# Segmented attention with memory beside a gated feed-forward: a new load order at the start, K of the first segment in two parts, recall in two halves, and a new written-out order

## Chip, core and metric

One Trainium2 chip, one core. The metric is device time of one execution in microseconds (us). Every instruction belongs to one engine: PE (TensorE; PEld is its weight load), DVE (VectorE), ACT (ScalarE), POOL (GpSimd) and SP (SyncE, which issues the transfers). Each engine runs its own queue in order.

## What is computed

The input x has 2048 rows of 512. Half A is attention with 32 heads of 16 over four segments of 512 rows, with a memory M that is carried from segment to segment; half B is a feed-forward of width 1792. A gate per row mixes the two.

```
q, k, v = x @ wq, x @ wk, x @ wv              # 32 heads of 16, 4 segments of 512
for s in range(4):
    p     = softmax(q[s] @ k[s].T * scale + causal_mask);  a_dot = p @ v[s]
    a_mem = (phi(q[s]) @ M) / (phi(q[s]) @ z + 1e-6)
    o[s]  = sigmoid(beta) * a_mem + (1 - sigmoid(beta)) * a_dot
    M, z  = M + phi(k[s]).T @ v[s],  z + phi(k[s]).sum()
a = concat(o) @ wo
b = (relu(x @ W_gate) * (x @ W_up)) @ W_down
out = sigmoid(x . gate_w) * a + (1 - sigmoid(x . gate_w)) * b
```

Inputs and outputs are bf16; phi(t) is t + 1 where t > 0 and exp(t) elsewhere.

## The kernel before, in words

**Tiling.** A unit is four pairs of heads (128 channels) of one segment: 4 units in each of the 4 segments. For each unit the kernel projects Q and K (`proj_q`, `proj_k`, transposed, 128 x 512 each, four matmuls over the four 128-row pieces of x), and for each segment four tiles of V (`proj_v`). x arrives transposed in `xT`: for segment 0 its first half of columns is turned on PE (`x0_tasks`, against an identity), its second half by a DMA transpose; later segments come by DMA transposes alone.

**Scores.** `score` (L636 and L649) runs four row tiles of PE side by side: each uses 32 rows and 128 columns of the array. A visit fills PSUM banks 0 to 3 (128 x 2048 f32), and one ACT instruction (L658) takes the exponential of all of it. The next visit writes the same banks, so it waits for that exponential. There are 72 visits: four of ordinary blocks per unit (2 matmuls in each of 4 row tiles), and one of diagonal blocks per two units (8 in each, L649). POOL masks the blocks (L687), DVE the diagonal ones (L669).

**Products and memory.** `pv` (L709) multiplies the exponentials with V in column tiles (128 rows, 32 columns of the array), `dens` (L765) and `memory` (L829) too. `recall` (L805) multiplies phi(q) with M in 16 tiles of 32 x 32, for all four units of a segment at once: 16 matmuls, each with 512 columns to stream, into four banks. `normalise` and the lines after it bring a unit's result to `oT` on DVE.

**The rest.** `ffn_tasks` makes gate and up (L478 or L482), Relu on ACT (L873) and the product on DVE (L879); `out_tile` adds `W_down` and `wo` in one bank, scales it on DVE (L905) and stores it (L910). These and the projections go through `full`: either as one matmul with 128 x 128 weights (L478), or as four with 32 columns of weights each, side by side (L482). One such quad does what one full matmul does.

**The order.** Nothing is scheduled on the chip. Every piece of work is a `Task`, in a `Plan`; the string `ORDER` gives the order in which all tasks are emitted, `UNITS` which buffer or PSUM bank each one takes. `Plan.run` walks through it. It also decides which of the two forms `full` takes: the quad form only if the last task with a mode of its own was one in column tiles.

```
            if t.eng == "PE":
                t.col = bool(t.flex) and mode == "col"
                mode = mode if t.col else t.mode
```

**The start.** `heat` (L924) keeps PE busy on constants, then the turns of x (L515), one filler matmul on zeros (L524), and Q of segment 0. The loads of SP's queue stand in this order: half of x's first rows, wq's piece 0, the DMA transpose of x's second half (L304), wq's pieces 2 and 3 (L306), wk in two halves, wv, the feed-forward weights by pieces, the rest of x. ACT's queue issues the other half of x and wq's piece 1. `LANDS` holds arrival times for the planner that made `ORDER`; the emitted kernel doesn't use them.

Of the kernel before, what the change touches and what calls it, by code (L numbers as in the profile page):

```python
# [12 lines left out]
P = 128  # L13
# [13 lines left out]
RQ = 5  # L27
RH = 14

ORDER = """  # L30
# [99 lines left out]
class Plan:  # L130

    def __init__(self):
        self.tasks, self.free = [], {}
# [9 lines left out]
    def add(self, *a, **k):  # L143
        t = Task(*a, **k)
        t.n = len(self.tasks)
        self.tasks.append(t)
        return t
# [32 lines left out]
def kernel(  # L180
# [492 lines left out]
    def attention(seg, c):  # L673
# [17 lines left out]
        if c % 2 == 0:  # L691
            diag(seg, c)
# [298 lines left out]
```

## Time and profile before

| | |
|---|---|
| time, median of 3 runs | 263.75 us (263.46 to 264.06) |
| profiled execution, span from first to last instruction | 261.6 us |
| granted TensorE clock | 0.998 |
| busy PE / DVE / ACT / POOL | 254.8 / 203.4 / 183.3 / 64.2 us |

The profiled execution has no time of its own beside its span; 2.1 us lie between the span and the median of the runs. In the views, a row of the timeline is: start, length, engine, line, operation, output from inputs, shapes, count; in brackets the idle time before and what ended it. Lengths of matmuls overlap, so the spacing of starts is what a matmul costs. About 30 of 3800 matmuls have no record, so a count can be one short.

### The profile page before, as it was taken

To read this page: it belongs to the slowest core of one execution; us is meant where nothing else is said; L and a number is where in the kernel's file an instruction comes from. 1 tells how busy PE (TensorE), PEld (TensorE's weight loads), DVE (VectorE), ACT (ScalarE), POOL (GpSimd) and SP (SyncE) were. 2 spreads that over 40 slices of the span, in tenths; PEclk is the share of its full clock that TensorE was granted. 3 is DMA by queue.
4 is the path that set the end of the run, shared out by engine and by line. 5 is a ranking of instruction groups with operands and counts; after the bars stand their busy time and mean duration, and the time that the engine had idled before them with its cause. 6 is when DMAs were issued, how large, how long until landed. Compare 5 with 4: busy or idle time off the path is not lost.

```text
span 261.6 us, 8758 instructions
## 1 busy us (share of the span) xinstructions
PE 254.8 (97%) x3769; PEld 117.2 (45%) x3798; DVE 203.4 (78%) x472; ACT 183.3 (70%) x168; POOL 64.2 (25%) x168
## 2 busy tenths in 40 slices
PE   8999999999999999999999999999999999999995
PEld 3444444454444454544444444445444344445454
DVE  2799999889896766948989868858988678788622
ACT  3199998998877788787768576878486768972000
POOL 8023462313322223322112222122122232120000
PEclk9999999999999999999999999999999999999999
DMA  7999885021311202100210500140200100230011
GB/s 193 305 289 283 214 262 109 4 43 23 84 34 43 89 25 80 36 0 3 84 21 3 95 4 26 58 142 3 80 4 23 32 5 23 98 107 3 3 43 40
DMA packets 31565, 19.71 MB, mean 75 GB/s; under 512 B 16040, under 2 KB 29992, under 8 KB 31528
## 3 DMA queue, kind: packets, MB, share of 16 engines
q1 hardware_dynamic: 31112, 18.90, 26.3%
q8 instruction: 29, 0.48, 0.8%
q10 hardware_dynamic: 416, 0.26, 0.3%
q14 instruction: 8, 0.07, 0.1%
HBM read 13.21 MB, written 2.55 MB: 60 GB/s over the span
## 4 chain that ended last, share of the span: by engine, by line
PE 90%; DVE 5%; DMA 1%; issue 1%; SPq 1%; ACT 0%; DVEq 0%; ACTq 0%
PE ps L478 54%; PE ps L482 19%; PE ps L636 8%; PE ps L709 7%; DMA wq_sb<-in_A_wq_dram 1%; PE ps L649 1%; DVE ktr L585 1%; DVE KT L588 1%; PE ps L829 1%; SPq L304 1%; DVE QT L569 0%; PE ps L765 0%; DVE T L740 0%; DVE hT L879 0%; PE ps L805 0%
## 5 line engine op out<-in xcount | busy, mean ns | idle before, releaser
L658 ACT ACTIVATE E<-ps 128x2048 bf16<-128x2048 f32 x64 | 120.1, 1877 | 32.0 <-PE ps L636 21.8
L687 POOL TENSOR_SCALAR_AFFINE_SELECT E<-E 128x256 bf16<-128x256 bf16 x128 | 55.6, 458 | 170.0 <-ACT E L658 169.9
L879 DVE TENSOR_TENSOR hT<-ps,rgr 128x512 bf16<-128x512 f32 x56 | 37.8, 684 | 13.1 <-PE ps L478 8.4
L478 PE MATMUL ps<-xT,wu_sb 128*128 128x512 bf16 x163 | 45.6, 380 | 0.7 <-issue 0.5
L873 ACT ACTIVATE rgr<-ps 128x512 bf16<-128x512 f32 x56 | 32.6, 596 | 15.3 <-PE ps L482 8.2
L478 PE MATMUL ps<-wd_sb,hT 128*128 128x512 bf16 (+1 forms) x174 | 41.7, 354 | 0.6 <-issue 0.5
L478 PE MATMUL ps<-xT,wg_sb 128*128 128x512 bf16 x149 | 40.9, 380 | 0.3
L740 DVE STREAM_TRANSPOSE T<-ps 128x512 f32<-128x512 f32 x32 | 22.2, 706 | 6.8 <-PE ps L709 6.6
L636 PE MATMUL ps<-QT,KT 32*128 32x320 bf16 (+3 forms) x512 | 25.4, 273 | 0.3
L478 PEld LDWEIGHTS <-wu_sb 128*128 128x128 bf16 x170 | 15.3, 98 | 19.4 <-issue 3.0
L478 PEld LDWEIGHTS <-hT 128*128 128x128 bf16 x178 | 15.6, 98 | 17.6 <-issue 2.1
L905 DVE TENSOR_SCALAR osr<-ps,ngcol 128x512 bf16<-128x512 f32 (+2 forms) x18 | 12.3, 691 | 13.3 <-PE ps L482 9.1
L478 PEld LDWEIGHTS <-wg_sb 128*128 128x128 bf16 x156 | 14.3, 98 | 17.8 <-issue 2.1
L709 PE MATMUL ps<-E,Vp 128*17 128x320 bf16 (+3 forms) x512 | 19.3, 273 | 0.0
L636 PEld LDWEIGHTS <-KT 32*128 32x128 bf16 x512 | 7.6, 92 | 25.7 <-issue 24.6
L658 ACT ACTIVATE Em<-ps 128x2048 bf16<-128x2048 f32 x8 | 15.0, 1874 | 5.0 <-PE ps L649 5.0
L482 PE MATMUL ps<-xT,wg_sb 128*32 128x512 bf16 x272 | 17.8, 379 | 0.0
L482 PE MATMUL ps<-wd_sb,hT 128*32 128x512 bf16 (+1 forms) x296 | 16.9, 359 | 0.0
L478 PE MATMUL ps<-wv_sb,xT 128*128 128x512 bf16 x59 | 16.7, 380 | 0.2
L478 PE MATMUL ps<-xT,wq_sb 128*128 128x512 bf16 x57 | 15.9, 382 | 0.5 <-DMA wq_sb<-in_A_wq_dram 0.4
L478 PE MATMUL ps<-xT,wk_sb 128*128 128x512 bf16 x54 | 15.3, 379 | 0.2 <-issue 0.2
L482 PE MATMUL ps<-xT,wu_sb 128*32 128x512 bf16 x216 | 15.0, 379 | 0.0
(100 smaller groups left out, 293.7 us busy)
## 6 DMA issues: line engine op xcount, KB each, us to landing
out_dram<-osr SPq DMA_DIRECT2D x15, 128.0 KB
wd_sb<-in_B_W_down_dram SPq DMA_DIRECT2D x2, 896.0 KB
xn<-in_A_x_dram SPq DMA_DIRECT2D x3, 512.0 KB
cdr<-coefs SPq DMA_DIRECT2D x6, 256.0 KB
xn<-coefs SPq DMA_DIRECT2D x6, 256.0 KB
wg_sb<-in_B_W_gate_dram SPq DMA_DIRECT2D x2, 512.0 KB
wu_sb<-in_B_W_up_dram SPq DMA_DIRECT2D x2, 512.0 KB
wg_sb<-in_B_W_gate_dram SPq DMA_DIRECT2D x2, 384.0 KB
```

The source lines that it names most:

```text
L304: nc.sync.dma_start_transpose(out=xT[0][:, NC // 2:NC, :], in_=x[0:L, halves[1]])
L478: nc.tensor.matmul(out, lhsT=lhsT, rhs=rhs, start=start, stop=stop)
L482: nc.tensor.matmul(out[r], lhsT=lhsT[:, r], rhs=rhs, start=start, stop=stop, tile_position=(0, 32 * j))
L585: d = plan.add("DVE", 600, key - RQK, lambda: nc.vector.tensor_copy(ktr[ks.i][:], bank(sl)), [a], DVL + 40, need=[ks], frees=[sl])
L636: nc.tensor.matmul(ps[:, j * L + o:j * L + o + L - q], lhsT=KT[i][rows, kb, 3 * r:3 * r + 2].rearrange("p h q -> p (h q)"), rhs=QT[i][rows ...
L658: last_exp[0] = [plan.add("ACT", 66 + 4 * L / 1.2, key, lambda: nc.scalar.activation(dst, ps[:, 0:4 * L], ACT.Exp, scale=SCALE), [a] + war ...
L687: nc.gpsimd.affine_select(out=m[:, :, o:o + HP], in_=m[:, :, o:o + HP], compare_op=ALU.is_ge, fill=0.0, base=HP, pattern=[[0, 4], [1, HP]] ...
L709: nc.tensor.matmul(bank(sl)[32 * m:32 * m + HW, q:q + w], lhsT=(Vp[i] if n < 4 else Vm)[:, kb, r, 4 * c + j, 0:HW], rhs=rhs, start=(n == 0 ...
L740: done.append(plan.add("DVE", 633, key - RL, lambda r=r, sl=sl: nc.vector.transpose(T[ts.i][:, r], bank(sl)), [a] + done, 75 if r else 0, ...
L873: r = plan.add("ACT", 478, key - RL, lambda sl=gsl, rs=rs: nc.scalar.activation(rgr[rs.i][:], bank(sl), ACT.Relu), [g], ACL, frees=[gsl])
L879: nc.vector.tensor_tensor(hT[hs1.i][:], bank(sl), rgr[rs.i][:], ALU.mult)),
L905: nc.vector.tensor_scalar(osr[os.i][:, n0 - c0:n1 - c0], bank(sl)[:, 0:n1 - n0], ngcol[:, tt:tt + 1], None, ALU.mult)),
```

## The change

- **Loads.** On SP's queue the first half of wk and then wq's pieces 2 and 3 now stand ahead of the DMA transpose of x's second half; the second half of wk stands behind it. The number and sizes of the loads are the same.
- **K of segment 0 in two parts.** The new `ORDER` puts on PE: Q from x's first two pieces (8 matmuls), K from the same two pieces (8), Q of three units from the other two (6), K from the other two (8), then V, the last unit's Q (2), gate and up. The first score visit stands behind 46 full matmuls; it stood behind 34.
- **Banks.** The four turns of x and the filler have PSUM banks of their own (4, 3, 5, 2 and 7).
- **Forms.** A stretch of PE work between two visits (or recalls) is now taken as a whole: if any task in it is in column tiles, all of its flexible tasks are quads. 375 full matmuls take the quad form; 246 did.
- **Recall** is emitted in two halves of 8 matmuls (two units each), which the order places apart.
- **Scores** go through a general `visit`; with `SIZES = [4] * 72` and `BANKS = [range(4)] * 72` each visit has the same matmuls in the same order as before.
- **Buffers and waits.** KT has 4 buffers for 5, ktr 4 for 3; the overwriting of QT and KT waits for the visits that read them, and not for `pv`. The 20 small copies of `row_gates` go from DVE to POOL.
- **Order.** `ORDER` and `UNITS` are new throughout. In the new one the instructions on PE between two visits are 10 full matmuls in 28 places, and 9 quads with two denominator groups in two places; before, the shortest were 10 full matmuls, in 3 places.

```diff
+RK = 4
...
             if t.eng == "PE":
-                t.col = bool(t.flex) and mode == "col"
-                mode = mode if t.col else t.mode
+                if t.mode in ("row", "quad"):
+                    settle()
+                else:
+                    stretch.append(t)
...
+        def settle():
+            col = any(t.mode == "col" for t in stretch)
+            for t in stretch:
+                t.col = bool(t.flex) and col
+            stretch.clear()
...
-    KT = [sb([P, 4, 5, P // 2], BF16, f"KT{i}") for i in range(RQ)]
+    KT = [sb([P, 4, 5, P // 2], BF16, f"KT{i}") for i in range(RK)]
...
-    ktr = ring([P, L], BF16, "ktr", 3)
+    ktr = ring([P, L], BF16, "ktr", 4)
...
     got_q = [load_wq(nc.sync, 0), load_wq(nc.scalar, 1)]
+    got_k = [load_rows(nc.sync, wk_sb, A_wk, 0, "k")]
+    nc.sync.dma_start(out=wq_sb[:, 2:NC, :],
+                      in_=A_wq.rearrange("(c p) n -> p c n", p=P)[:, 2:NC, :])
     nc.sync.dma_start_transpose(out=xT[0][:, NC // 2:NC, :], in_=x[0:L, halves[1]])
     got_x0b = arrival("x0")
-    nc.sync.dma_start(out=wq_sb[:, 2:NC, :],
-                      in_=A_wq.rearrange("(c p) n -> p c n", p=P)[:, 2:NC, :])
     got_q += [arrival("q%d" % ci) for ci in range(2, NC)]
-    got_k = [load_rows(nc.sync, wk_sb, A_wk, i, "k") for i in range(2)]
+    got_k.append(load_rows(nc.sync, wk_sb, A_wk, 1, "k"))
...
-        nc.vector.tensor_copy(gcat[rows, 1], g[rows, 1, :, m])
+        nc.gpsimd.tensor_copy(gcat[rows, 1], g[rows, 1, :, m])
         for c in range(NC):
-            nc.vector.tensor_copy(gcat[rows, 0, c], g[rows, 0, c, (m + c) % 4])
+            nc.gpsimd.tensor_copy(gcat[rows, 0, c], g[rows, 0, c, (m + c) % 4])
...
-                sl = work()
+                sl = plan.one("ps", ((4, 3, 5, 2)[2 * ci + t],))
...
-                    js = work()
+                    js = plan.one("ps", (7,))
...
-        war = [att.get(("pv", u - RQ)), att.get(("recall", u - RQ))]
+        old = u - RQ
+        war = [att.get(("score", old)), att.get(("score", old // 2 * 2, "d"))]
+        pwar = [att.get(("recall", old)), att.get(("denpe", old // 4, old % 4 // 2))]
...
-        a = plan.add("PE", 266, key, pe, [prj["pq", seg, c] for c in range(NC)]
-                     + [att["mbd", seg - 1]] + [(b, 3900.25) for b in loads], PEL, need=sls,
-                     mode="quad", size=16)
+        for half in range(2):
+            cs = (2 * half, 2 * half + 1)
...
+            a = plan.add("PE", 133, key + half, pe, [prj["pq", seg, c] for c in cs]
+                         + [att["mbd", seg - 1]] + [(loads[c], 3900.25) for c in cs], PEL,
+                         need=[sls[c] for c in cs], mode="quad", size=8)
...
+    SIZES = [4] * 72
+    BANKS = [range(4)] * 72
```

More of the change, by code (lines that the diff above doesn't have):

```diff
@@ L565, in proj_q @@
         else:
[L566 removed]
+            a = matmuls(key, list(got_q) + [(w, 0.25) for w in war if w], sl, proj_mm(wq_sb, c, seg),
                         chunk={ci: got_x[seg][ci // 2] for ci in range(NC)})
@@ L573, in proj_q @@
             prj["pq", seg, c] = plan.add("DVE", 730, key + 500, lambda: phi(
-                pqT[i][:], QT[i][:], ex1[es.i][:]), [b], DVL, frees=[es],
+                pqT[i][:], QT[i][:], ex1[es.i][:]), [b] + pwar, DVL, frees=[es],
                 lock=True)
     def proj_k(seg, c):
+        plan.tag = "qk" if seg else "qk0"
         i, u, sl = seg % 2, 4 * seg + c, work()
         key = K(4 * seg + c - 2 - (2 if seg else 0), 10)
-        war = [att.get(("pv", u - RQ)), att.get(("recall", u - RQ))]
-        a = matmuls(key, war, sl, proj_mm(wk_sb, c, seg),
+        old = u - RK
+        war = [att.get(("score", old)), att.get(("score", old // 2 * 2, "d"))]
+        a = matmuls(key, [(w, 0.25) for w in war if w], sl, proj_mm(wk_sb, c, seg),
                     chunk={ci: got_x[seg][ci // 2] + [got_k[ci // 2]] for ci in range(NC)})
@@ new lines, in item @@
+    def item(u, f, j):
+        rows = slice(32 * j, 32 * j + 32)
+        if f == "d":
+            for v in range(2):
+                i = (u + v) % RQ
+                for kb in range(4):
+                    yield (KT[(u + v) % RK][rows, kb, 2:4], QT[i][rows, kb * P:kb * P + HP],
+                           4 * HP * v + HP * kb, HP)
+        else:
+            i, r = u % RQ, f % 2
+            for kb, q, o in PIECES[f // 2]:
+                yield KT[u % RK][rows, kb, 3 * r:3 * r + 2], QT[i][rows, q:L], o, L - q
@@ new lines, in target, with visit, pe @@
+    def target(u, f, j0, j1):
+        if f == "d":
+            return Em[:, j0:j1].rearrange("p j v k q -> p (j v k q)")
+        return E[(NFILL * u + f) % RE][:, j0 * L:j1 * L]
+    def visit(items, key, banks):
+        mm, busy = [], [0.0] * 4
+        for n, (u, f, j) in enumerate(items):
+            for lhsT, rhs, o, w in item(u, f, j):
+                mm.append((busy[j], j, n, lhsT, rhs, banks[n] * L + o, w))
+                busy[j] += w + 6
+        mm.sort(key=lambda m: m[:3])
+        def pe():
+            for _, j, _, lhsT, rhs, o, w in mm:
+                nc.tensor.matmul(ps[:, o:o + w], lhsT=lhsT.rearrange("p h q -> p (h q)"), rhs=rhs,
+                                 start=True, stop=True, tile_position=(32 * j, 0))
+        runs = []
+        for n, (u, f, j) in enumerate(items):
+            if (runs and runs[-1][1:3] == [u, f] and runs[-1][4] == j and n - runs[-1][0] < CUT
+                    and banks[n] == banks[n - 1] + 1):
+                runs[-1][4:6] = j + 1, n + 1
+            else:
+                runs.append([n, u, f, j, j + 1, n + 1])
+        sls = [Slot([tuple(("ps", b) for b in banks[n0:n1])]) for n0, _, _, _, _, n1 in runs]
+        deps = []
+        for u, f in dict.fromkeys(it[:2] for it in items):
+            for w in ((u, u + 1) if f == "d" else (u,)):
+                deps += [prj["q", w // 4, w % 4]] + prj["k", w // 4, w % 4]
+        a = plan.add("PE", max(busy) / 2.4 + 17, key - QKP, pe, deps, 275, mode="row", need=sls, size=16)
+        for (n0, u, f, j0, j1, n1), sl in zip(runs, sls):
+            if f == "d":
+                att["score", u, "d"] = a
+                wars = [att[k] for k in (("pv", u - 1), ("pv", u - 2)) if k in att]
+            else:
+                wars = eread.get(NFILL * u + f - RE, [])
+                att["score", u] = a
+            rd = max(sum(w + 6 for _, _, _, w in item(u, f, j1 - 1)) * (1 + (n1 > 4)), 0) / 2.4 + 17
+            exps.setdefault((u, f), []).append(plan.add(
+                "ACT", 66 + (n1 - n0) * L / 1.2, key,
+                lambda n0=n0, n1=n1, u=u, f=f, j0=j0, j1=j1: nc.scalar.activation(
+                    target(u, f, j0, j1), ps[:, banks[n0] * L:(banks[n0] + n1 - n0) * L], ACT.Exp,
+                    scale=SCALE), [(a, 275 - max(0.0, max(busy) / 2.4 + 17 - rd))] + wars, ACL, frees=[sl]))
@@ L799, in recall @@
                 .to_broadcast([8, 16, L])), [att["coefs", seg, c // 2]] + war, 4200, xfer=1850.0))
-        def pe():
-            for c in range(NC):
-                for j, m in turned(c):
-                    rows = slice(32 * j, 32 * j + 32)
-                    nc.tensor.matmul(bank(sls[c])[32 * m:32 * m + 32],
-                                     lhsT=mbd[i][rows, c].rearrange("p r e -> p (r e)"),
-                                     rhs=pqT[units[c] % RQ][rows, :], start=True, stop=True,
-                                     tile_position=(32 * j, 32 * m))
@@ L912, in out_tile, with FILLS, score @@
             1400 if tt == NT - 1 else 2400, frees=[os], xfer=400.0)
+    def FILLS(u):
+        return [0, 1, 2, 3] + ["d"] * (u % 2 == 0)
+    tape = [(u, f, j) for u in range(4 * NSEG) for f in FILLS(u) for j in range(4)]
+    tape_done, seen = set(), [0, 0]
+    def score():
+        v, n = seen
+        items = tape[n:n + SIZES[v]]
+        seen[:] = v + 1, n + len(items)
+        visit(items, KA(items[0][0] - LEAD, AUNIT * (n % 18) / 18), BANKS[v])
+        tape_done.update(it[:2] for it in items if it[2] == 3)
+    CUT = 4
+    SIZES = [4] * 72
+    BANKS = [range(4)] * 72
     OTW, OBANKS, MEMGAP = 3, (7, 6), 1600.25
```

130 lines of the change are left out of this document (57 added, 73 removed), and 126 rows, old and new, of the table ORDER.

## Prediction

> **What bounds the kernel now.** I read the page first, then who waits on PE, then the start and single visits in the timeline.
>
> ```profile
> PE 254.8 (97%) x3769; PEld 117.2 (45%) x3798; DVE 203.4 (78%) x472; ACT 183.3 (70%) x168; POOL 64.2 (25%) x168
> PE   8999999999999999999999999999999999999995
> PEclk9999999999999999999999999999999999999999
> PE 90%; DVE 5%; DMA 1%; issue 1%; SPq 1%; ACT 0%; DVEq 0%; ACTq 0%
> ```
>
> PE is busy for 254.8 of 261.6 us at the full granted clock, in every slice but the first and the last, and 90% of the chain that ended last is PE. The waits of PE alone, all of them:
>
> ```profile
> PE ps L478 <- issue: 1.4, 9, 0.2
> PE ps L924 <- PEq L975: 0.8, 1, 0.8
> PE ps L478 <- DMA wq_sb<-in_A_wq_dram: 0.4, 1, 0.4
> ```
>
> One wait for data (0.4 us), the launch, and 1.4 us of "issue" in nine places, of which the rivals speak. So no engine is waited for behind the start: the kernel costs what PE's instructions cost one after the other. A visit shows that price.
>
> ```profile
> 26.89 0.40 PE L636 MATMUL ps<-QT,KT 32*128 32x448 bf16 x8
> 27.22 1.04 PE L478 MATMUL ps<-wv_sb,xT 128*128 128x512 bf16 x4
> 28.09 0.59 PE L478 MATMUL ps<-xT,wk_sb 128*128 128x512 bf16 x2
> 28.52 0.59 PE L478 MATMUL ps<-wv_sb,xT 128*128 128x512 bf16 x2
> 28.95 0.59 PE L478 MATMUL ps<-xT,wk_sb 128*128 128x512 bf16 x2
> 29.48 0.40 PE L636 MATMUL ps<-QT,KT 32*128 32x448 bf16 x8
> ```
>
> Ten full matmuls stand between two scores. From 27.22 to 28.95 eight of them take 1.73 us, 0.216 each. The last two start at 28.95 and the next score at 29.48: 0.53 us, where two matmuls are 0.43. So 0.10 us goes where PE changes from 128 x 128 weights to the scores' row tiles. From one score to the next it is 2.59 us.
>
> **The change, part by part.**
>
> *Start.* The chain of waits and PE's timeline:
>
> ```profile
> 1.82 1.31 SPq L304
> 3.19 3.65 DMA wq_sb<-in_A_wq_dram
> 4.55 1.97 PE L478 MATMUL ps<-xT,wq_sb 128*128 128x512 bf16 x8
> 6.89 1.90 PE L478 MATMUL ps<-xT,wq_sb 128*128 128x512 bf16 x8 [0.36 <-DMA wq_sb<-in_A_wq_dram]
> 8.62 2.75 PE L478 MATMUL ps<-xT,wk_sb 128*128 128x512 bf16 x12
> ```
>
> The DMA transpose takes 1.31 us of SP's queue, wq's second half is issued behind it at 3.19 and lands 3.65 us later, at 6.84. The first eight Q matmuls run from 4.55 to 6.52. One is 0.38 long (the row at 28.95: 0.59 for two, less one spacing), so the eighth starts at 6.14 and the ninth could at 6.36 or 6.37. It starts at 6.89: **0.52 us** are lost. That is all that the new start can give back: behind 6.89 PE runs on without a wait.
>
> With the change PE wants at 6.37 wk's first half, 8 matmuls later (8.09) both wq's second half and x's second half, 6 later (9.39) wk's second half. Each load here is 256 KB. Rates:
>
> ```profile
> 1.90:3.50 1.60, 1.60 (x6) 0.50 (x5) 0.00 (x0) 1.25 (x1) 1.54 (x2) 1.00 0.87 274
> 3.50:5.00 1.50, 1.50 (x13) 1.12 (x12) 0.85 (x2) 0.74 (x2) 1.48 (x6) 1.00 1.18 270
> 5.00:6.84 1.84, 1.53 (x8) 0.49 (x5) 0.00 (x0) 0.00 (x0) 1.32 (x9) 1.00 0.94 274
> ```
>
> (The last column is GB/s.) At 274 GB/s 256 KB take 0.96 us, and the fourth group of 256 KB (x's rows, wq's front, the transpose, wq's rest) would be through at 1.9 + 3.83 = 5.73; it landed at 6.84, 1.1 later. By that measure the third group lands at 5.9, the fifth at 7.8, the sixth at 8.7. Now wk's first half is third (wanted 6.37), the transpose fifth (8.09), wk's second half sixth (9.39): 0.5, 0.3 and 0.7 us of room. I take the 0.52 us as gained and 0 to 0.3 us as given back, 0.05 of it in the sum. The first score then stands at 4.63 + 46 x 0.216 + 0.10 = 14.66. Its K and Q pass through ten DVE operations behind 9.8 us; the casts go at 0.62 us each:
>
> ```profile
> 7.96 2.48 DVE L569 CAST QT<-ps 128x512 bf16<-128x512 f32 x4 [3.19 <-PE ps L478]
> 12.28 0.28 DVE L588 TENSOR_SCALAR KT<-ktr,mcol_e 128x256 bf16<-128x256 bf16 x1
> 12.60 0.12 PEld L636 LDWEIGHTS <-KT 32*128 32x128 bf16 x8 [0.42 <-DVE KT L588]
> ```
>
> Six casts (3.7 us) and four masked copies at about 0.25 make 4.5, so 14.4: in time. Moving full matmuls from behind the first score to ahead of it costs nothing, they are the same ones.
>
> *Recall in halves.*
>
> ```profile
> 122.13 1.03 PE L478 MATMUL ps<-xT,wg_sb 128*128 128x512 bf16 x4
> 123.09 0.43 PE L805 MATMUL ps<-pqT,mbd 32*32 32x512 bf16 x16
> 123.46 1.47 PE L478 MATMUL ps<-xT,wg_sb 128*128 128x512 bf16 x6
> ```
>
> Four fulls from 122.13 end at 122.99; recall starts at 123.09 (0.10 for the change of tiles), and 0.37 us pass to the next full: 0.10 to change back and 0.27 for the pass, in which 16 tiles stream 512 columns side by side. Before: 0.10 + 0.27 + 0.10 = 0.47 a segment. A half streams the same 512 columns through eight tiles. Sixteen starts lie within 0.05 us (0.43 in all, less the 0.38 of one); eight of them fall away: 0.245 for a half. In the new order each half lies with one side at a score and the other at ordinary matmuls. The ordinary side's change (0.10) replaces that which the score had there; new is the change s between score tiles (32 x 128) and recall tiles (32 x 32). So a segment has 2 x (0.245 + s) against 0.47: +0.02 + 2s. The trace has no such pair. The bounds: s = 0, or the dearest change that it has. The nearest is one that alters the columns alone:
>
> ```profile
> 255.98 0.61 PE L482 MATMUL ps<-wo_sb,oT 128*32 128x256 bf16 x16
> 256.52 0.95 PE L478 MATMUL ps<-wd_sb,hT 128*128 128x128 bf16 x14
> ```
>
> Four quads of 256 columns (0.109 each, half of 0.216) end at 256.42, the full form starts at 256.52: 0.10. So s lies between 0 and 0.10, and all three segments cost **+0.06 to +0.68 us**; I take s = 0.10 and +0.62, since both kinds of change, of rows alone (fulls to scores) and of columns alone, cost that. The Trainium skill, "TensorEngine Tiling (Array Packing)", Key Properties, says that changing the tiling mode, and not just the tile, drains the engine; by that s is a full change and the sum that with s = 0.10. The changes of other pairs in this trace (0.10 each) speak for it; no run here shows this pair.
>
> *Forms.* 129 more fulls become quads.
>
> ```profile
> 244.74 3.19 PE L482 MATMUL ps<-wd_sb,hT 128*32 128x512 bf16 x56
> 247.76 0.60 PE L482 MATMUL ps<-wo_sb,oT 128*32 128x512 bf16 x8
> ```
>
> 56 matmuls, 14 quads, take 3.02 us: 0.216 each, as a full. So nothing, and at a rounding of 0.001 us either way 0.1. The changes of tile shape around scores stay: 72 into the visits and 72 out of them, in the old order and in the new; only their partners differ (full before a visit 51 times, now 44). The visits themselves are the same instructions.
>
> *Buffers, banks, POOL's copies.* No row of PE's waits names a bank, QT, KT or ktr, so looser waits have nothing to remove. The small copies leave DVE:
>
> ```profile
> L404 DVE COPY gcat<-gall x16: 149/152/376, 23.6 to 29.1; 32x2 f32<-32x2 f32 x16
> ```
>
> Twenty at 0.15 are 3 us of DVE. On POOL, busy for 64 of 261.6 us, they lie beside everything; the first user is the first unit's `normalise`. Zero; without that cover its two banks stay held for up to 3 us longer.
>
> **Sum.** -0.52 + 0.05 + 0.62 = +0.15 on the span of 261.6; the tail behind PE is the same three operations. What lies around the span doesn't change, so 263.75 + 0.15 = **263.9 us**.
>
> **The rivals.**
>
> *Recall's tiles change for nothing* (s = 0): -0.52 + 0.05 + 0.06, 263.3 us. Against it stand the two kinds of change above.
>
> *The lost time comes back at the start* or where segment 1's x is read. In the order V of segment 1 stands at about 21.9; before it stood behind 25. Its transpose is issued until 17.97:
>
> ```profile
> 11.83 6.14 SPq L274 DMA_TRANSPOSE xT<-in_A_x_dram  x1
> 18.00:19.50 1.50, 1.45 (x14) 0.60 (x14) 1.47 (x5) 1.50 (x3) 0.73 (x2) 1.00 1.25 277
> ```
>
> With 512 KB at 277 GB/s, 1.9 us, and the 1.1 us that stragglers took above, it lands near 21: 1 us of room. If the loads come 0.3 to 0.5 us later than I reckon: 264.3 us.
>
> *The scores' own chain becomes the bound (slower).* Score, exponential, next score is a loop through PE and ACT over the same four banks:
>
> ```profile
> 96.02 0.40 PE L636 MATMUL ps<-QT,KT 32*128 32x320 bf16 x8
> 96.55 1.88 ACT L658 ACTIVATE E<-ps 128x2048 bf16<-128x2048 f32 x1 [0.36 <-POOL E L687]
> 27.34 1.88 ACT L658 ACTIVATE E<-ps 128x2048 bf16<-128x2048 f32 x1
> ```
>
> Score to exponential 0.45 to 0.53 us, exponential 1.88, then the hand-over w to PE. The exponential from 27.34 ends at 29.22 and the next score starts at 29.48, at its counted place, so w is at most 0.26. The loop is then 2.39 + w at a start delay of 0.51, against 2.59 for ten fulls: it decides when w is over 0.20. The new order has 28 such visits for 3, and two of 2.50 us (two denominator groups and nine quads; with ten, from 96.02 to 98.74 below, it is 2.72). At w = 0.26 it costs 28 x 0.06 + 2 x 0.15 = 2.0 us; at 0.23, the middle of where it decides, 28 x 0.03 + 2 x 0.12 = 1.1: 265.0 us. For it: the order leaves no reserve. Against it: the one hand-over that PE is seen to wait for, from DVE's KT (ends 12.56) to its load at 12.60, takes 0.05, and at that w there are 0.15 us of room. Where the order puts two or more other ACT operations into a short visit (six times) a longer visit follows.
>
> *Fewer bursts of instructions help PE* (or: the "issue" waits are real and go): -1.4 us, 262.5 us. Against it:
>
> ```profile
> 98.74 0.40 PE L636 MATMUL ps<-QT,KT 32*128 32x320 bf16 x8
> 99.29 0.81 PE L478 MATMUL ps<-xT,wu_sb 128*128 128x512 bf16 x3 [0.16 <-issue]
> 101.76 0.41 PE L649 MATMUL ps<-QT,KT 32*128 32x64 bf16 x32
> ```
>
> This visit takes 3.02 us, 0.43 more than one of ten fulls, so twelve fulls fit without any gap; the trace records eleven. The gap is a matmul without a record, not a stall.
>
> **How the numbers follow.** Forecast (263.9) 0.44; recall free (263.3) 0.12; start or x late (264.3) 0.14; the scores' loop (265.0) 0.21; bursts (262.5) 0.09. A measurement of this kernel tells about 0.2%, 0.53 us, from no change. Within it: 0.44 + 0.12, less 0.03 for luck below it, + 0.05 of the late loads: 0.58. Slower: the loop 0.21 and 0.09 of the late loads, 0.30. Faster: 0.09 + 0.03, 0.12. The range goes from 263.0 (recall free and nothing given back, 263.2, less 0.2 of the 0.3 by which the runs shown lie beside their median) to 265.0, the middle of the loop's price; bursts and half of the loop lie outside, 0.2.
>
> **What would show it.** Right: PE's first Q and K matmuls without a DMA wait between 4.55 and 14.7; the first score near 14.7; each recall row 8 matmuls and some 0.24 us plus 0.10 on either side; 2.59 us between scores with ten fulls. Wrong: recall to score starts 0.24 us apart (s = 0); a DMA wait at 6.4, 8.1 or 21.9; score rows that wait for ACT's E, 2.6 us apart or more with ten fulls; a PE sum off by more than 1 us, which would mean that quads or visits cost something else in their new neighbourhood.

## The result and the profile after

The changed kernel takes 264.07 us (median of 20 runs, 263.63 to 264.75), the kernel before 263.71 us (20 runs, 263.26 to 264.19). The medians lie 0.36 us apart. The ratio is 1.0015, 95% interval 1.0008 to 1.0022, which makes 0.40 us, between 0.21 and 0.58. The profiled execution took 263.85 us, its span is 262.1 us (before: 261.6). In all executions of the experiments below, the time is 1.66 to 2.04 us over the span, 1.72 in the middle, so the span of 261.6 belongs to an execution of about 263.3 us, one of the quickest of the kernel before (an estimate): the two traces may differ by more than the medians do.

The page of the changed kernel, busy times and the chain that ended last:

```profile
PE 255.4 (97%) x4158; PEld 120.0 (46%) x4185; DVE 202.1 (77%) x452; ACT 181.7 (69%) x168; POOL 68.9 (26%) x188
PE 96%; DVE 2%; issue 1%; DVEq 0%
```

The picture is that of before: PE is busy for 97% of the span and makes up nearly all of the chain that ended last. The small copies went from DVE to POOL and PE doesn't wait for them. All of PE's waits (line, releaser, us, times, longest):

```profile
PE ps L491 <- issue: 2.1, 13, 0.2
PE ps L989 <- PEq L1040: 0.8, 1, 0.8
PE ps L491 <- DVE grc L481: 0.2, 1, 0.2
```

The wait for wq is gone from the list. The row with DVE's `grc` is a matmul without a record: the visit around it has exactly its counted length.

PE's timeline at the start, one row of the kernel before and then the changed kernel:

```profile
3.46 1.06 PE L515 MATMUL ps<-ident,xn 128*128 128x128 bf16 x8
```

```profile
3.67 1.05 PE L529 MATMUL ps<-ident,xn 128*128 128x128 bf16 x8
4.75 1.93 PE L491 MATMUL ps<-xT,wq_sb 128*128 128x512 bf16 x8
6.52 1.89 PE L491 MATMUL ps<-xT,wk_sb 128*128 128x512 bf16 x8
8.24 1.46 PE L491 MATMUL ps<-xT,wq_sb 128*128 128x512 bf16 x6
9.54 1.89 PE L491 MATMUL ps<-xT,wk_sb 128*128 128x512 bf16 x8
14.82 0.40 PE L682 MATMUL ps<-QT,KT 32*128 32x448 bf16 x8
```

Q, K, Q, K follow one another without a wait. But the turns of x start at 3.67; before, they started at 3.46, and the first Q matmul at 4.55 instead of 4.75. The first score stands at 14.82, 2.21 us later than before (12.60) with 12 more full matmuls ahead of it, which are 2.59 us. So the start gives **0.38 us**; the forecast had 0.47. Of the 0.52 us of the wait, 0.14 are given back: the first Q matmul starts 0.20 us later, and 0.05 of that come back, most of it since the slow phase of the first matmuls takes 0.04 us less from Q ("The slow first matmuls" below).

A visit of ten full matmuls, one score to the next:

```profile
17.41 0.40 PE L682 MATMUL ps<-QT,KT 32*128 32x448 bf16 x8
20.00 0.40 PE L682 MATMUL ps<-QT,KT 32*128 32x320 bf16 x8
```

2.59 us, as counted, and so are all visits of ten full matmuls; the two of nine quads with two denominator groups take 2.50 us each, as counted too. The scores' loop holds none of them up.

The two halves of recall of the second segment with memory:

```profile
143.93 0.40 PE L682 MATMUL ps<-QT,KT 32*128 32x448 bf16 x8
144.26 0.41 PE L851 MATMUL ps<-pqT,mbd 32*32 32x512 bf16 x8
144.60 2.12 PE L491 MATMUL ps<-wd_sb,hT 128*128 128x512 bf16 x9
146.64 0.41 PE L851 MATMUL ps<-pqT,mbd 32*32 32x512 bf16 x8
146.98 0.40 PE L682 MATMUL ps<-QT,KT 32*128 32x448 bf16 x8
```

From a half to what follows it there are 0.34 us, to a full matmul or to a score alike. Visits with a half are 0.338 us longer than the same visits without, six times: 2.03 us, where three whole recalls took 3 x 0.47 = 1.41. That is **+0.62 us**, and s, the price of the change between score tiles and recall tiles, is 0.338 - 0.245 = 0.09.

One stall was not in the forecast. DVE and PE behind the products with V at 56 us:

```profile
56.39 1.28 DVE L781 STREAM_TRANSPOSE T<-ps 128x512 f32<-128x512 f32 x2
56.56 0.61 PE L495 MATMUL ps<-xT,wu_sb 128*32 128x512 bf16 x8
57.13 0.61 PE L495 MATMUL ps<-xT,wg_sb 128*32 128x512 bf16 x8
57.56 0.62 PE L495 MATMUL ps<-xT,wu_sb 128*32 128x512 bf16 x8
```

Two quads take 0.43 us (57.13 to 57.56); from 56.56 to 57.13 there are 0.57. The gate's first quad goes into the bank that the first of the two transposes reads; that ends at 57.08, and the quad's instruction waits for DVE's semaphore. The stall costs **0.15 us**. The list of waits doesn't name it (it puts idle time down only where it sees an end, and the ends of matmuls are modelled); the spacing of the starts does.

The account, from the starts of matmuls in both traces, up to the last matmul:

| term | forecast | traces |
|---|---|---|
| wait for wq's rest goes | -0.52 | -0.52 |
| given back at the start | +0.05 | +0.14 |
| recall in halves | +0.62 | +0.62 |
| wait for a bank at 57 us | 0 | +0.15 |
| memory and V products beside other neighbours | 0 | +0.07 and +0.05 |
| sum | +0.15 | +0.51 (the spans: +0.52) |

The row of the neighbours is counted so: memory's matmuls lengthened three visits by 0.50 us each before and by 0.50, 0.53 and 0.55 now, and a pair of V products costs 1.112 us behind quads against 1.108 ahead of them, eleven times.

### The profile page after: what moved, and what is told of

Same layout as the page of the kernel before. It is cut to its first block, busy times and chain, and to the rows that moved or that the text cites. A ratio compares the mean times of both kernels' runs of the same rounds, so it can differ in the third digit from the quotient of the medians.

```text
span 262.1 us, 9502 instructions
## 1 busy us (share of the span) xinstructions
PE 255.4 (97%) x4158; PEld 120.0 (46%) x4185; DVE 202.1 (77%) x452; ACT 181.7 (69%) x168; POOL 68.9 (26%) x188
## 4 chain that ended last, share of the span: by engine, by line
PE 96%; DVE 2%; issue 1%; DVEq 0%
PE ps L491 47%; PE ps L495 30%; PE ps L682 9%; PE ps L750 6%; PE ps L989 1%; PE ps L851 1%; DVE T L781 1%; PE ps L876 1%; PE ps L529 0%; PE ps L807 0%; DVE hT L927 0%; DVE QT L586 0%; DVE omr L862 0%; DVE osr L954 0%; DVE grc L481 0%
## 5 line engine op out<-in xcount | busy, mean ns | idle before, releaser
L491 PE MATMUL ps<-xT,wu_sb 128*128 128x512 bf16 x130 | 36.0, 380 | 1.1 <-issue 0.8
L491 PE MATMUL ps<-xT,wg_sb 128*128 128x512 bf16 x134 | 36.3, 380 | 0.4 <-DVE grc L481 0.2
L495 PE MATMUL ps<-wd_sb,hT 128*32 128x512 bf16 (+1 forms) x516 | 30.8, 368 | 0.0
L682 PE MATMUL ps<-QT,KT 32*128 32x64 bf16 (+3 forms) x768 | 28.7, 245 | 0.1
L491 PE MATMUL ps<-wd_sb,hT 128*128 128x512 bf16 (+1 forms) x117 | 25.1, 341 | 0.8 <-issue 0.8
L495 PE MATMUL ps<-xT,wu_sb 128*32 128x512 bf16 x344 | 23.3, 380 | 0.0
L495 PEld LDWEIGHTS <-hT 128*32 128x32 bf16 x516 | 12.8, 97 | 10.9 <-issue 1.1
L491 PEld LDWEIGHTS <-hT 128*128 128x128 bf16 x123 | 10.1, 98 | 11.1 <-issue 2.4
L586 DVE CAST QT<-ps 128x512 bf16<-128x512 f32 x16 | 10.8, 680 | 5.3 <-PE ps L491 4.6
L562 ACT ACTIVATE ex<-ktr 128x512 bf16<-128x512 bf16 x12 | 7.4, 627 | 8.3 <-DVE ktr L604 7.0
```

Of the source, the lines that this page charges most:

```text
L491: nc.tensor.matmul(out, lhsT=lhsT, rhs=rhs, start=start, stop=stop)
L495: nc.tensor.matmul(out[r], lhsT=lhsT[:, r], rhs=rhs, start=start, stop=stop, tile_position=(0, 32 * j))
L562: return es, plan.add("ACT", 520, key + 500, lambda: nc.scalar.activation(ex1[es.i][:], src(), ACT.Exp), [a], ACL, need=[es])
L586: prj["q", seg, c] = plan.add("DVE", 600, key - RQK, lambda: nc.vector.tensor_copy(QT[i][:], bank(sl)), [a] + war, DVL, frees=[sl])
L682: nc.tensor.matmul(ps[:, o:o + w], lhsT=lhsT.rearrange("p h q -> p (h q)"), rhs=rhs, start=True, stop=True, tile_position=(32 * j, 0))
```

## The experiments

Theory A is this account. Its rivals are named with each run. All times are device medians; ratios are to the kernel before, which ran beside each, so a run is compared with the changed kernel by the ratios (1.0015 for that one). Each trace is of one execution.

### The start

`old_start`: the loads and the first matmuls as before, in the changed kernel.

```diff
-    got_k = [load_rows(nc.sync, wk_sb, A_wk, 0, "k")]
+    nc.sync.dma_start_transpose(out=xT[0][:, NC // 2:NC, :], in_=x[0:L, halves[1]])
     nc.sync.dma_start(out=wq_sb[:, 2:NC, :],
                       in_=A_wq.rearrange("(c p) n -> p c n", p=P)[:, 2:NC, :])
-    nc.sync.dma_start_transpose(out=xT[0][:, NC // 2:NC, :], in_=x[0:L, halves[1]])
+    nc.sync.dma_start(out=wk_sb[:, 0:2, :],
+                      in_=A_wk.rearrange("(c p) n -> p c n", p=P)[:, 0:2, :])
...
-ORDER: ... 73 6 105 91 63 77 7 74 75 76 102 103 104 8 60 61 92 ...
+ORDER: ... 73 6 7 74 75 76 102 103 104 60 61 105 91 63 77 8 92 ...
```

> The changed kernel with the loads and the first matmuls of the kernel before: DMA transpose, wq's pieces 2 and 3, wk in two halves; on PE the six Q matmuls on pieces 2 and 3 stand ahead of the first K matmuls. All else as changed. Theory A (two effects at the start: the wait of 0.52 us goes, but the two loads that now stand ahead of the transpose delay x's own first rows by 0.2 us): the turns of x start at 3.46 again and not at 3.67, PE waits for wq about 0.5 us ahead of the ninth Q matmul, the first score stands 38 matmuls behind 6.89, at 15.2 instead of 14.82, and the span is 0.37 us longer than that of the changed kernel. Rival B (x's rows were late by chance in that one execution): the turns start at 3.46 to 3.67 whatever the load order, and the new start is worth the whole 0.5 us.

264.60 us, ratio 1.0028 (1.0016 to 1.0040): 0.13% above the changed kernel, 0.34 us, and the intervals overlap. PE's timeline:

```profile
3.46 1.06 PE L531 MATMUL ps<-ident,xn 128*128 128x128 bf16 x8
4.55 3.98 PE L493 MATMUL ps<-xT,wq_sb 128*128 128x512 bf16 x14
8.38 3.62 PE L493 MATMUL ps<-xT,wk_sb 128*128 128x512 bf16 x16
15.38 0.40 PE L684 MATMUL ps<-QT,KT 32*128 32x448 bf16 x8
```

The turns start at 3.46 again, and the first score is 0.56 us later than in the changed kernel (I expected 0.37). Behind the first score both traces are the same to 1 ns (244.18 us to the last matmul). But there is no wait for wq: the 14 Q matmuls take 3.83 us from 4.55 to 8.38, where 14 at 0.216 are 3.02. The first four take some 0.42 us each. So something slowed PE and filled the wait; that is taken up below. The 0.56 us are therefore not the price of the wait alone.

`mid_transpose`: the transpose between wk's first half and wq's rest.

```diff
-    got_k = [load_rows(nc.sync, wk_sb, A_wk, 0, "k")]
+    nc.sync.dma_start(out=wk_sb[:, 0:2, :],
+                      in_=A_wk.rearrange("(c p) n -> p c n", p=P)[:, 0:2, :])
+    nc.sync.dma_start_transpose(out=xT[0][:, NC // 2:NC, :], in_=x[0:L, halves[1]])
     nc.sync.dma_start(out=wq_sb[:, 2:NC, :],
                       in_=A_wq.rearrange("(c p) n -> p c n", p=P)[:, 2:NC, :])
-    nc.sync.dma_start_transpose(out=xT[0][:, NC // 2:NC, :], in_=x[0:L, halves[1]])
...
```

> The changed kernel with one load moved: the DMA transpose stands between wk's first half and wq's pieces 2 and 3 (wk half, transpose, wq rest, wk half). Theory A: only one load of 256 KB competes with x's first rows, so the turns of x start between 3.46 and 3.67, near 3.55; the transpose lands near 7, wq's rest before 8.1; PE has no wait and gains 0 to 0.2 us on the changed kernel. Rival: the rest of wq is late (it is issued 1.3 us later) and lands behind 8.2; PE waits for it and the gain is eaten.

264.33 us, ratio 1.0015 (1.0004 to 1.0026).

```profile
3.46 0.69 PE L533 MATMUL ps<-ident,xn 128*128 128x128 bf16 x8
4.43 1.89 PE L495 MATMUL ps<-xT,wq_sb 128*128 128x512 bf16 x8 [0.17 <-ACT xT L548]
8.44 1.47 PE L495 MATMUL ps<-xT,wq_sb 128*128 128x512 bf16 x6 [0.40 <-DMA wq_sb<-in_A_wq_dram]
```

x's rows were on time, and wq's rest was not: the rival's case. The ninth Q matmul could have started at 7.88 and started at 8.44, so 0.56 us were lost (the row counts 0.40 of it as idle). More is lost here than was won: the first score stands at 15.02, 0.2 us later than in the changed kernel.

`act_queue`: wk's first half on ACT's queue; on SP's the transpose, then wq's rest, as before.

```diff
-    got_k = [load_rows(nc.sync, wk_sb, A_wk, 0, "k")]
+    nc.scalar.dma_start(out=wk_sb[:, 0:2, :],
+                        in_=A_wk.rearrange("(c p) n -> p c n", p=P)[:, 0:2, :])
+    nc.sync.dma_start_transpose(out=xT[0][:, NC // 2:NC, :], in_=x[0:L, halves[1]])
     nc.sync.dma_start(out=wq_sb[:, 2:NC, :],
                       in_=A_wq.rearrange("(c p) n -> p c n", p=P)[:, 2:NC, :])
-    nc.sync.dma_start_transpose(out=xT[0][:, NC // 2:NC, :], in_=x[0:L, halves[1]])
...
```

> The changed kernel with another way of issuing the loads at the start: wk's first half goes out on ACT's queue behind wq's second piece, and SP's queue issues the DMA transpose, wq's pieces 2 and 3, wk's second half, as in the kernel before. Theory A (what delays x's rows is the second load of 256 KB ahead of the transpose): the turns of x start at 3.46, wk's first half lands near 6, wq's rest near 7.2 (wanted at 7.9), the transpose near 6, PE has no wait for a load, and the first score comes 0.2 to 0.3 us earlier than in the changed kernel, apart from how long the first matmuls run at half speed. Rival B: wk's half delays x's rows as much from ACT's queue, or the table load that it pushes back delays ACT's casts of x: the turns or the first Q matmul come 0.2 us later and nothing is gained.

264.03 us, ratio 1.0020 (1.0010 to 1.0030), so nothing is gained.

```profile
3.54 1.05 PE L533 MATMUL ps<-ident,xn 128*128 128x128 bf16 x8
4.62 2.35 PE L495 MATMUL ps<-xT,wq_sb 128*128 128x512 bf16 x8
6.81 1.89 PE L495 MATMUL ps<-xT,wk_sb 128*128 128x512 bf16 x8
57.80 0.61 PE L499 MATMUL ps<-xT,wg_sb 128*32 128x512 bf16 x8 [0.30 <-DVE T L785]
```

There is no wait for a load, but eight Q matmuls take 2.19 us instead of 1.73, and the bank at 57 us is waited for 0.48 us instead of 0.15. That wk's first half was in time is owed to the slow Q matmuls, which put off the first K matmul to 6.81: in act_gate, further down, with the same loads and no slow Q matmul, PE waits for it.

Over all thirteen traces, x's turns start at 3.67 to 3.71 in the four with both loads ahead of the transpose; at 3.46 in mid_transpose, with one of them ahead; at 3.46, 3.46, 3.52 and 3.74 with the transpose first; at 3.54 to 3.70 with wk on ACT's queue. The pattern is Theory A's for the two loads, but the one 3.74 shows that the same rows can be as late by themselves. That wk's and wq's loads delay x's rows is therefore likely and not shown.

### Recall

`before_halves`: in the kernel before, recall of two segments in halves.

```diff
+        first, mate = {1: ((1, 2), 881), 2: ((2, 3), 1043)}.get(seg, (range(NC), None))
-        def pe():
-            for c in range(NC):
+        def pe(cs=first):
+            for c in cs:
...
+        late[mate] = lambda: pe([c for c in range(NC) if c not in first])
...
             t.emit(t.col) if t.flex else t.emit()
+        if t.n in late:
+            late[t.n]()
```

> The kernel before with one part of the change alone: the recalls of segments 1 and 2 are emitted in two halves of 8 matmuls, with two to eight ordinary full matmuls between the halves; nothing else moves. Theory A (a half costs 0.245 us of its own, ten hundredths less than nothing saved, plus every change of tiles it brings): each half stands between full matmuls and costs 0.245 + 0.10 + 0.10, a segment 0.89 instead of 0.47, so the stretch from the first score to the last matmul grows by 0.84 us and the time too. Rival B (the halves cost no more than the whole, and the 0.61 us of the changed kernel come from where they stand, beside the scores): the stretch stays within 0.1 us.

264.62 us, ratio 1.0045 (1.0028 to 1.0061).

```profile
123.11 0.41 PE L809 MATMUL ps<-pqT,mbd 32*32 32x512 bf16 x8
123.45 1.47 PE L478 MATMUL ps<-xT,wg_sb 128*128 128x512 bf16 x6
124.85 0.41 PE L809 MATMUL ps<-pqT,mbd 32*32 32x512 bf16 x8
125.19 0.60 PE L478 MATMUL ps<-xT,wq_sb 128*128 128x512 bf16 x2
```

The two visits with recall grew by 0.418 us each and no other by over 0.02; the stretch from first score to last matmul grew from 245.88 to 246.72 us, 0.84, as Theory A has it. Rival B falls: the split itself costs, wherever the halves stand. A half between full matmuls costs (0.47 + 0.42) / 2 = 0.445 us, beside a score 0.338, so a score beside it saves one change of tiles (0.107) and no more.

### The bank at 57 us

`gate_bank`: one DVE task moved.

```diff
-ORDER: ... 409 387 52 190 189 191 192 ...
+ORDER: ... 409 387 190 189 191 52 192 ...
```

> The changed kernel with one DVE task (two small operations that prepare the gate per row, 0.4 us) moved in the order from ahead of the pair of transposes at 56.4 us to behind them. Theory A (the gate quads at 57.13 wait 0.15 us for the bank that the first transpose frees at 57.08): the transpose ends near 56.6, the eight quads behind it follow the ones before at 0.22 us, from score to score it takes 2.72 us instead of 2.87, and the span is 0.15 us shorter. Rival B (the 0.15 us is the price of quads behind products with V in that order, no wait): the visit still takes 2.87 us.

264.18 us, ratio 1.0014 (0.9999 to 1.0029): the times don't tell it from the changed kernel. The trace does. DVE and PE there:

```profile
55.88 0.70 DVE L779 STREAM_TRANSPOSE T<-ps 128x512 f32<-128x512 f32 x1
56.55 0.61 PE L493 MATMUL ps<-xT,wu_sb 128*32 128x512 bf16 x8
56.99 0.60 PE L493 MATMUL ps<-xT,wg_sb 128*32 128x512 bf16 x8
```

The transpose ends at 56.58, the quads follow at 0.22 us each, and the visit takes 2.72 us instead of 2.87. Rival B, that the 0.15 us were the price of quads in that place, falls: it was a wait, and 0.15 us is its price. The span is 0.13 us shorter.

### The scores' loop

`short_visits`: three scores earlier on PE.

```diff
-ORDER: ... 753 311 754 461 ...   898 1041 668 1042 819 823 833 834 ...   1215 1217 1216 1209 1210 1159 ...
+ORDER: ... 753 311 461 754 ...   898 819 833 1041 668 1042 823 834 ...   1215 1159 1217 1216 1209 1210 ...
```

> The changed kernel with three scores moved up in the order, so that three visits of ten full matmuls become shorter and the next ones longer by as much: the visit at 69.5 us gets 8, that at 154.6 gets 8, that at 217.4 gets 6. By PE's work alone they would take 2.16, 2.16 and 1.73 us. This measures the hand-over w from the end of an exponential to the next score, on which my rival of the scores' loop rested. Theory A (w is small, at most 0.11, since the visits of 2.50 us ran at their counted length): all three take the length of the loop, 2.39 + w, between 2.4 and 2.5 us, whatever their matmuls, and the whole is about 1.2 us slower. Rival B (w is over 0.2, and the visits of ten matmuls already wait a little): they take 2.6 us and the whole is 1.8 us slower.

265.74 us, ratio 1.0067 (1.0044 to 1.0089). The score rows at the three places, and ACT's row between the middle two:

```profile
69.99 0.40 PE L680 MATMUL ps<-QT,KT 32*128 32x320 bf16 x8
72.43 0.40 PE L680 MATMUL ps<-QT,KT 32*128 32x320 bf16 x8 [0.21 <-ACT E L705]
155.37 0.40 PE L680 MATMUL ps<-QT,KT 32*128 32x320 bf16 x8
155.82 1.88 ACT L705 ACTIVATE E<-ps 128x2048 bf16<-128x2048 f32 x1 [0.18 <-PE ps L680]
157.74 0.40 PE L680 MATMUL ps<-QT,KT 32*128 32x448 bf16 x8
218.41 0.40 PE L680 MATMUL ps<-QT,KT 32*128 32x320 bf16 x8
220.87 0.40 PE L680 MATMUL ps<-QT,KT 32*128 32x320 bf16 x8 [0.66 <-ACT E L705]
```

From score to score there are 2.44, 2.38 and 2.46 us, with eight, eight and six full matmuls, where the matmuls alone would take 2.16, 2.16 and 1.73: this is the loop's own length, and rival B's 2.6 us is out. The exponential ends at 157.70, the score starts at 157.74, so w, the hand-over from ACT to PE, is 0.04. Visits of ten full matmuls (2.59) have 0.13 to 0.22 us to spare. The stretch behind the first score grew by 1.23 us, as expected.

### Mended versions

`act_gate`: act_queue and gate_bank in one.

> act_queue and gate_bank together: the changed kernel with both of its own losses mended that I found, the late rows of x and the wait for a bank at 57 us; what is left of the loss is recall in halves and the dearer neighbours of memory and V products. Theory A: 0.12 us (bank) and 0.2 to 0.3 us (start) better than the changed kernel, 263.7 us, the same as the kernel before within 0.1%.

264.12 us, ratio 1.0021 (1.0011 to 1.0031), where the same time as before was expected: missed, in two places. At the start no Q matmul is slow, and PE waits for wk's first half. It could have gone on at 6.35, so 0.33 us are lost, and the first score stands at 14.99, 0.17 us later than in the changed kernel. The bank's wait stays away (the visit takes 2.77 us), but the visit behind it has a gap inside memory's 64 matmuls:

```profile
6.68 1.90 PE L493 MATMUL ps<-xT,wk_sb 128*128 128x512 bf16 x8 [0.17 <-DMA wk_sb<-in_A_wk_dram]
59.86 0.22 PE L878 MATMUL ps<-Vp,pK 128*32 128x34 bf16 x6 [0.26 <-issue]
```

The instruction at 59.86 waits for no semaphore, and the visit is 0.43 us longer. One execution shows it. So ACT's queue is no cure for the start: wk's half, wanted at 6.35, comes too late there.

`before_early_k`: the new start alone, in the kernel before, with wk's first half on ACT's queue. Five tasks get other banks, listed in the last line.

```diff
+    nc.scalar.dma_start(out=wk_sb[:, 0:2, :],
+                        in_=A_wk.rearrange("(c p) n -> p c n", p=P)[:, 0:2, :])
...
+    nc.sync.dma_start(out=wk_sb[:, 2:4, :],
+                      in_=A_wk.rearrange("(c p) n -> p c n", p=P)[:, 2:4, :])
...
+ORDER: ... 101 7 63 91 77 5 4 6 60 61 62 74 75 76 88 89 90 102 103 8 64 65 92 93 78 79 9 114 115 ... 121 128 219 122 116 ...
+banks: 77 in 0, 219 in 5, 222 in 4, 228 in 5, 231 in 4
```

> The kernel before with the new start alone, in the form of act_queue: wk's first half on ACT's queue; on PE six K matmuls on x's first two pieces between the first eight Q matmuls and the rest of Q; one tile of V (two matmuls) is taken ahead of the first score and two of the next tile move up one visit; some PSUM banks differ for that. Recall whole, forms, order behind the start as before. Theory A: the wait of 0.52 us for wq goes and about 0.1 of it comes back in front of the first score, where DVE's casts of Q and K now start later; the last matmul comes 0.3 to 0.4 us earlier than in the kernel before: 263.4 us. Rival B (DVE's casts and masks, which start 0.7 us later, end after 13.1): the first score waits for DVE, and the gain is gone or turned round.

264.61 us, ratio 1.0040 (1.0027 to 1.0053). The gain is turned round, as rival B said, but the first score doesn't wait for DVE; other waits took the place:

```profile
23.24 0.59 PE L480 MATMUL ps<-xT,wg_sb 128*128 128x512 bf16 x2 [0.66 <-DVE hT L881]
```

The first score stands at 12.78, 0.17 us later than before, and 0.24 us ahead of it are lost to wq's rest at 7.92. Behind it, the bank of a product that DVE reads late held PE 0.8 us at 23, and a bank of V 0.2 at 14.

`before_early_k2`: that product two rows earlier on DVE, the V matmuls at the visit's end.

```diff
-ORDER: ... 117 222 ...  48 ... 46 ... 47 ... 49 ... 227 ... 230 ...
+ORDER: ... 223 117 ...  48 ... 46 ... 227 230 47 49 ...
```

> before_early_k with two waits of my own making taken out: one product of gate and up moves on DVE ahead of two rows of the gate's sum, so that its bank is free 0.8 us earlier, and the two V matmuls that moved up one visit stand at its end. Theory A: the stretch from the first score to the last matmul is 0.43 us shorter than that of the kernel before (two full matmuls fewer in it) instead of 0.61 us longer, the first score stands at about 12.8 against 12.6, and the time is 0.2 us below that of the kernel before: 263.5 us. Rival B (DVE, which starts its casts 0.2 to 0.7 us later in this order, is the limit for the first 25 us): another wait for DVE takes the place and nothing is gained.

264.45 us, ratio 1.0025 (1.0015 to 1.0036). Rival B has it again: the second visit is 0.43 us shorter than before, as meant, but 0.28 us were lost at 25, where PE waits for DVE, and 0.36 at 33, where the trace names nobody. In this execution the first eight Q matmuls took 2.71 us, and the first score stands at 13.61.

```profile
4.76 2.87 PE L480 MATMUL ps<-xT,wq_sb 128*128 128x512 bf16 x8
25.49 0.59 PE L480 MATMUL ps<-xT,wg_sb 128*128 128x512 bf16 x2 [0.22 <-DVE hT L881]
```

No version here beats the kernel before.

### The slow first matmuls

In the traces above, matmuls start 0.43 us apart (512 columns) or 0.107 (128 columns) up to a point between 3.6 and 6.8 us, and 0.216 or 0.055 from then on. For that, the first eight Q matmuls cost between nothing (five kernels) and 0.98 us (before_early_k2) more than 1.73. To see what this is worth, I cut the matmuls on constants that run ahead, in both kernels. Theory C: the slow phase gets longer, and the kernel before hides part of it in its wait for wq, the changed one none. Its rival: both grow by the same.

```diff
-        for k in range(7):
+        for k in range(6, 7):
```

> The kernel before without six of the seven matmuls on constants that keep PE busy from 0.84 to 3.4 us. The traces so far show the first matmuls at half speed (0.43 us apart instead of 0.22) until a point that differs from run to run, 3.6 to 6.2 us. Theory C (in the kernel before, the wait for wq's second half hides up to 0.5 us of that; in the changed one there is no such wait and every slow matmul counts): without the early matmuls PE is slow until 6.5 to 8.5 us, the eight Q matmuls take up to 3.4 us instead of 1.7, the wait for wq (till 6.89) is filled by them, and the time grows by 0.5 us less than that of the changed kernel with the same cut: +0.8 to +1.3 us. Rival (the speed has nothing to do with the work before): the time stays the same.

264.63 us, ratio 1.0028 (1.0013 to 1.0043).

> The changed kernel with the same cut (one of seven matmuls on constants left). Theory C: the slow matmuls stand on the path in full, so the time grows by 0.4 to 0.5 us more than that of the kernel before with the same cut: +1.2 to +1.8 us on the changed kernel. Rival: it grows by the same amount in both.

265.29 us, ratio 1.0062 (1.0042 to 1.0081). The first rows of PE of before_no_heat, then of after_no_heat with an ACT row from further on:

```profile
4.81 5.55 PE L478 MATMUL ps<-xT,wq_sb 128*128 128x512 bf16 x16
```

```profile
4.77 3.03 PE L491 MATMUL ps<-xT,wq_sb 128*128 128x512 bf16 x8
7.64 1.89 PE L491 MATMUL ps<-xT,wk_sb 128*128 128x512 bf16 x8
53.43 1.88 ACT L707 ACTIVATE Em<-ps 128x2048 bf16<-128x2048 f32 x1 [1.69 <-PE ps L491]
```

In the first, nine Q matmuls are slow and the tenth in part, until about 8.7 us. The ninth starts at 8.20, long after wq's rest landed in the trace of before (6.84), and the wait for wq is gone: it was filled. There are 1.85 us more of slowness than in the trace of before, and the first Q matmul is 0.26 later; together they would have moved the first score by 2.1 us. It moved by 1.57 (to 14.18), so the 0.52 of the wait were absorbed. In the second, the slow phase ends at about 7.1 us, and every slow matmul moves K: there are 1.10 us more of slowness than in the trace of the changed kernel, the first Q matmul is 0.02 later, and the first score moved by 1.12 (to 15.94). So a slow phase of PE disappears in the wait of the kernel before and counts in full in the changed one, up to the length of the wait; one trace of each shows it.

The times grew by 0.28% and by 0.47% (1.0062 against 1.0015), 0.7 and 1.2 us, the difference on the side of Theory C. The ranges of the ratios overlap, the two slow phases were of different length, and the second profile holds a stall of 1.3 us at 53 us that comes from another place, so the size of the difference is not shown.

## Why the prediction was right, point by point

- **The outcome.** 263.9 was forecast and 264.07 measured: slower by 0.15%, within the 0.2% to which most of the chance went. The sign and the two large terms were right. The sum was 0.36 us short of the difference of the two traces and 0.21 short of that of the medians. Three terms were missed, all on the same side; that the total stayed in the expected band is owed to the band, which at 0.53 us is wider than what was missed.
- **Recall in halves** (+0.62): right, 0.62, though with s = 0.09 for the 0.10 taken. before_halves shows that it is the split that costs, and not the place. The Trainium skill's rule ("TensorEngine Tiling (Array Packing)", Key Properties) that a change of tiling mode drains the engine agrees: a change between score tiles and recall tiles costs what the others cost. The rival with s = 0 is out.
- **The start** (-0.52 + 0.05): the wait went and no load came late, as reckoned: K's first half was wanted at 6.52, wq's rest and the transpose at 8.24, and PE waited for none. The sum on DVE ahead of the first score was added up wrong: six casts and four copies at 0.25 are 4.7 us, not 4.5, which leaves DVE done at 14.5 and still ahead of the score. The term for what is given back was mis-sized, 0.14 for 0.05: I asked whether the moved loads would come in time, not whether they might delay the loads in front of them. x's rows were used 0.2 us later; that the moved loads did it is not shown. The length of the slow first matmuls was put at nothing. It happened to be nearly the same in the two traces (0.08 and 0.04 us), which is luck: other executions had up to 0.98.
- **"The scores' own chain becomes the bound"** (0.21): out. w is 0.04, as the hand-over from DVE suggested (0.05); the bound of 0.26 was the reach of one row, not a value.
- **x of segment 1 late** (0.14): out; no wait of PE for a load behind the start.
- **Bursts** (0.09): out as forecast; the "issue" rows went from nine to thirteen and the visits around them have their counted lengths. act_gate shows that a real gap of this kind exists, once.
- **Forms and visits at nothing**: quads cost what fulls do (two take 0.43 us), but memory's and V's neighbours cost 0.07 and 0.05. No run was made for these two; they are counted from the starts in both traces.
- **Buffers, banks at nothing**: this step failed. I looked only at whether looser waits could free something. The new order also took new banks, and one of them made a quad wait for a DVE transpose, 0.15 us. The step that was left out is to walk each bank from its last reader to its next writer, with the durations of before.

## What to carry to other kernels

When PE has no gaps, count its program: full matmuls, changes of tiles, passes. Splitting a short pass whose parts ran side by side cost nearly the whole pass again here (0.245 us a half, 0.27 the whole), plus the changes of tiles. And a wait near the start is worth less than its length: it also absorbs what comes late by chance, such as PE's slow first microseconds, so taking it away gains less than the trace of one execution promises. Whether the time gets less steady by it is not shown: from fastest to slowest run there were 1.1 us, and 0.9 before, but 1.6 in other runs of the same kernel before.

## What the runs showed of the hardware

- **PE's first matmuls run at half speed, and for how long differs from one execution to the next.** The same matmuls on constants from 0.84 us on were followed by full speed at about 3.6, 3.9, 4.1, 4.2, 4.4, 4.7, 4.8, 5.6, 5.9, 6.2 and 6.8 us in eleven traces. 3.9 and 6.8 belong to before_early_k and before_early_k2, whose programs are the same up to there. Without six of these matmuls it came at 7.1 and 8.7 us, later than in any of the eleven. The profile's column of the granted clock says 1.00 throughout; only the spacing of starts shows it. The Trainium skill, "TensorE: Matmul & The Clock Gate", Part 1, has the reason that fits: a free-running window of activity decides when the clock doubles, so the same kernel sees different numbers of slow matmuls; its spacings, 426.7 and 106.7 ns cold, are those of the traces. Its window of 3.4 us is not seen in full: the earliest switch came 2.8 us after the first matmul (3.6 less 0.84).
- **One place is unsteady.** Between 51 and 60 us, behind the DMA transpose of the third segment's x and while DVE is hardly ever idle, three traces of the new order have stalls of their own: DVE 0.8 us late at 52.5 and PE 0.5 in all (act_queue), a gap among memory's matmuls (act_gate), the exponential 1.7 us late and PE 1.3 (after_no_heat). Where a releaser is named, it was long done. In act_queue and after_no_heat the time passes between the end of a PE matmul and the semaphore event that tells of it: 0.87 us for a matmul that ends at 51.59 (act_queue) and 1.53 for a score that ends at 51.88 (after_no_heat), where the changed kernel's events here come 0.01 to 0.06 us behind the ends. In these two, and in no other trace of the new order, the DMA transpose of pK occupies SP's queue for 2.4 and 2.6 us at this place instead of 1.2, and the late instructions of DVE and ACT start 0.1 to 0.25 us ahead of its end. That is a lead and no more: what holds the events is open, no run was made for it, and act_gate's gap has no such sign. The first row is the changed kernel's, the second act_queue's:

```profile
50.97 1.20 SPq L620 DMA_TRANSPOSE pK<-pkT  x1
```

```profile
50.35 2.38 SPq L624 DMA_TRANSPOSE pK<-pkT  x1
```
